# Which VectorE step each GpSimd step waits for, in a gated linear attention with a feed-forward block

## The chip, the cores and the metric

The kernel runs on one core of a Trainium2 chip. The metric is the device time of one execution in microseconds (us). A core has TensorE (PE in the profile, with its weight loads as PEld), VectorE (DVE), ScalarE (ACT), GpSimd (POOL) and SyncE (SP, which here only issues DMAs).

## The reference

Two parts follow each other. The first is a linear attention whose state is turned and damped by a complex gate at every time step, for 4 batches, 8 heads, 768 steps and a head dimension of 48. The second normalises the 384 channels of each step and applies a feed-forward block of 1536 hidden channels with a residual.

```python
# q, k, v, a_re, a_im: (4, 8, 768, 48)
mag = np.sqrt(a_re * a_re + a_im * a_im)
scale = np.minimum(mag, 0.999) / (mag + 1e-06)
a_re_n, a_im_n = (a_re * scale, a_im * scale)
for t in range(S):
    ar, ai = a_re_n[:, :, t, :, None], a_im_n[:, :, t, :, None]
    new_re = ar * S_re - ai * S_im
    new_im = ar * S_im + ai * S_re
    kv = np.einsum('bhd,bhe->bhde', k[:, :, t], v[:, :, t])
    S_re, S_im = (new_re + kv, new_im)
    y[:, :, t] = np.einsum('bhd,bhde->bhe', q[:, :, t], S_re)
x = y.transpose(0, 2, 1, 3).reshape(B, S, H * D)
xn = (x - mean(x)) / np.sqrt(var(x) + 1e-06) * g_ln      # over the 384 channels
out = x + np.maximum(xn @ w_ch1, 0.0) @ w_ch2
```

## The kernel before

**Tiling.** The 768 steps of a batch are cut into 6 chunks of 128, and two chunks make a pair: 4 batches times 3 pairs give 12 pairs P = 0 to 11 and 24 chunks n = 0 to 23. The gates' running products are turned into sums: logarithms of the magnitudes (`l`) and angles (`th`) are added up along time by matmuls with triangles of ones (`dec`, `ph`), then turned back by exponentials (`e`, `en`) and sines (`sin`, `cos`). q and k are multiplied with these (`qe`, `ke`, then `qs`, `ks`), and attention inside a chunk is a masked matmul, with a state `G` carried from chunk to chunk.

**Steps and names.** The function `pair_ops` adds every step of a pair by a name, with what it needs. The names that this text uses, with P the pair, n the chunk, and a last digit for a half:

- `ln`, `iv` (L459, L461, ScalarE), `r` (L463, a product of two SBUF tiles), `r2` (L472, its square), `u` (L473, ScalarE), `l` (L477), `lc` (L480, a clamp in place), `dec` (L488, TensorE), `th` (L496, ScalarE), `ph` (L503 and L507, TensorE), `sin` (L525, ScalarE), `qt` (L532, TensorE), `abs` (L544), `car` (L520).
- `ke`, `qe`, `ks`, `qs`: products of two SBUF tiles. All `tensor_tensor` calls run through one helper, so that `r`, `r2`, `ke`, `qe`, `ks`, `qs`, `atm`, `gs` and `G` all stand under L295.
- `kT`, `qT` (L613, transposes on TensorE), `ksT`, `qsT` (L292, their evacuation from PSUM), `am` (L636), `atm` (L652, evacuation of `am` with the mask), `gm` (L660), `G` and `gs` (the state), `y` (L697 and L700), `bn` (L707, L708, statistics), `x` (L714 or L717), `xr` (L724, between SBUF tiles), `xtr` and `xT` (L734, L292), `rstd` (L753 and L755 on GpSimd: an addition and a power).
- `mm1`, `relu`, `mm2` (L767, L779 or L781, L791: the feed-forward block), `oa` and `ot` (L796, L807 or L805: the output), `st` (L813, the store).
- `v` (L414, a cast), `wl.0` and `wl.1` (L369, L371: loads of the two weight matrices w1b and w2b, issued on GpSimd), `wc` (L385, scaling of w1b in SBUF), and `pad`, `car0`, `zrow`, `pick`, `mask`, `ident`: constants set by GpSimd at the start.

**Order.** A text, `PLAN`, lists all 1088 steps in one order, each with its engine: V is VectorE, G is GpSimd, A ScalarE, P TensorE, S SyncE, and a digit behind it is the PSUM bank. Each engine works through its own steps in that order. `tile_gateloop__then__metaformer_identity_kernel` hands it to `Graph.run`, which emits the steps. The waits that the data and the buffers ask for are added on their own. Beside these, a token may end in `@step`: then the first instruction of that step also waits for the last instruction of the named one, although it needs nothing of it.

```python
where, _, ops[name].behind = where.partition("@")
...
for op in steps:
    if op.behind:
        tc.add_manual_dep(made[op.name][0], made[op.behind][-1].name, info,
                          reason="turns at the shared port")
```

GpSimd has 103 steps, and 54 of them carry such a mark. Their targets are VectorE steps of every kind: 9 times `atm`, 6 times `ksT`, 5 times `bn`, 4 times `qsT`, and others. Many targets are the VectorE step just ahead of one that works between SBUF tiles. Since GpSimd works in order, a wait also holds everything behind it on GpSimd.

Of the kernel before, what the change touches and what calls it, by code (L numbers as in the profile page):

```python
# [53 lines left out]
warm.w17:P5 e.0.1:A1 k.1.1:S warm.w12:P3 lc.0.0:V iv.2.0:A lc.1.0:V dec.0.0:P7 qe.0.1.0:G@lc.0.0 car.0.0:V6 dec.1.0:P4
q.1.0:S car.0.1:V0 en.0.1:A1 r.2.0:V qrow:G warm.w16:P2 en.0.0:A7 ph.1.0:P2 e.1.0:A4 q.2.1:S ke.0.0.0:V e.0.0:A7
warm.28:P1 are.3.0:S r2.2.0:V en.1.0:A4 warm.19:P7 warm.w4:P1 uthc:V ke.0.1.0:V vf.1.0:S u.2.0:A warm.w0:P5 qe.0.0.0:V
warm.w40:P4 warm.w22:P7 car.1.0:V2 warm.w3:P7 k.1.0:S warm.5:P7 warm.w20:P5 l.2.0:V warm.w31:P7 warm.w23:P5 aim.3.0:S
warm.w21:P7 warm.w28:P1 qe.1.0.0:V tab.trig.3:A sin.0.1:A0 sin.0.0:A6 lc.2.0:V qt.0.1:P0 ks.0.1.1:V sin.1.0:A2 row.0:S
# [10 lines left out]
cos.3.0:A0 wc.0.0:V mm1.0.1.1:P2 vf.2.1:S wc.0.2:V x.2:A7 wc.2.2:V mm1.0.0.1:P0 wc.2.0:V relu.0.1:A2 wc.2.1:V bn.3:V5
mm1.0.0.0:P0 qe.2.0.0:G@wc.2.1 xtr.2:P3 aim.5.0:S x.3:V5 mm1.0.2.0:P6 ke.2.0.0:G@bn.3 xT.2:V3 xtr.3:P5 mm1.0.2.1:P6  # L70
xT.3:V5 tab.log.6:A u.3.0:A gs.3:V4 mm1.1.0.1:P2 qs.2.0.0:V relu.0.2:A6 mm1.1.1.0:P4 ks.2.0.0:V relu.0.0:A0
mm1.1.1.1:P4 ks.2.0.1:V mm1.1.0.0:P2 l.3.0:V ln.4.0:A mm1.1.2.1:P0 relu.1.1:A4 relu.1.0:V2 kT.5:P6 mm1.1.2.0:P0
iv.4.0:A ksT.5:V6 qT.5:P4 relu.1.2:A0 lc.3.0:V qT.4:P3 r.4.0:G@ksT.5 qsT.5:V4 kT.4:P5 qsT.4:A3 dec.3.0:P6 ksT.4:V5
# [5 lines left out]
mm2.1.2:P6 xr.1:G@qe.3.0.1 q.4.0:S xT.5:V5 ke.3.0.1:G ot.3:V7 mm1.2.0.0:P4 ot.1:V6 mm1.2.0.1:P4 aim.6.0:S rstd.2:G
qs.3.0.0:V k.4.0:S mm1.2.2.0:P2 tab.trig.7:A th.4.0:A ke.3.0.0:V mm1.2.2.1:P2 k.4.1:S relu.2.0:A4 ks.3.0.0:V ph.4.0:P6  # L80
st.1:S relu.2.2:A2 st.3:S l.5.0:V qT.6:P0 q.4.1:S abs.4.0:A6 dps.4:P1 kT.6:P5 v.3:G@ks.3.0.0 qsT.6:V0 mm1.2.1.0:P2
are.7.0:S th.5.0:A decc.4:V1 ksT.6:V5 kT.7:P0 sin.4.0:A6 vf.4.0:S dps.3:P4 mm1.2.1.1:P2 decc.3:V4 car.4.0:A6 ksT.7:V0
qT.7:P5 relu.2.1:A2 lc.5.0:V am.6:P6 r.6.0:G@ksT.7 qsT.7:V5 gm.6:P4 ph.5.0:P0 cos.4.0:A atm.6:V6 vf.4.1:S G.6:A4
am.7:P2 sin.5.0:A0 gm.7:P4 q.5.0:S ke.4.0.0:G@atm.6 atm.7:V2 y.6:P5 mm2.4.0:P7 abs.5.0:A0 ke.4.0.1:G mm2.5.0:P6
th.6.0:A G.7:V4 q.5.1:S y.7:P2 bn.6:V5 cos.5.0:A qe.4.0.0:G@G.7 mm2.5.1:P6 are.8.0:S bn.7:V2 x.6:A5 mm2.5.2:P6
aim.7.0:S x.7:V2 mm2.4.1:P7 ks.4.0.0:V k.5.1:S xtr.7:P2 xtr.6:P5 mm2.4.2:P7 tab.log.8:A ln.7.0:A xT.7:V2 ksT.8:S
dec.5.0:P0 xT.6:V5 r2.6.0:A qs.4.0.0:V kT.9:P4 e.5.0:A0 mm1.3.1.0:P2 v.4:G@xT.6 aim.8.0:S ksT.9:V4 en.5.0:A0 qT.8:P5
# [6 lines left out]
th.7.0:A q.6.1:S qT.10:P4 qsT.11:V5 vf.5.1:S xtr.8:P6 xr.7:G@l.7.0 cos.6.0:A ph.7.0:P0 xT.8:V6 ke.5.0.0:G@qsT.11
xT.9:V7 th.8.0:A qsT.10:V4 dps.6:P2 mm1.4.1.0:P6 sin.7.0:A0 ot.7:V3 mm1.4.0.1:P4 st.7:S rstd.4:G decc.6:A2 ks.5.0.0:V
r2.8.0:A mm1.4.0.0:P4 k.7.0:S vf.6.1:S lc.7.0:V mm1.4.1.1:P6 ke.6.0.0:G relu.4.0:A4 car.7.0:V0 aim.9.0:S kT.10:P3
kT.11:P2 abs.7.0:A0 ksT.10:V3 mm1.4.2.0:P4 relu.4.1:A6 ksT.11:V2 q.7.0:S am.10:P0 ks.6.0.1:V dec.7.0:P2
ks.6.0.0:G@ksT.11 atm.10:V0 q.7.1:S am.11:P6 mm1.4.2.1:P4 atm.11:V6 tab.log.10:A en.7.0:A2 mm2.9.0:P1 v.5:G@atm.10
e.7.0:A2 mm2.9.1:P1 relu.4.2:V4 qe.6.0.0:G@atm.11 ln.9.0:A y.10:P0 row.7:S gm.10:P2 vf.7.0:S ph.8.0:P6 u.8.0:A
bn.10:V0 aim.10.0:S G.10:V2 iv.9.0:A xr.8:G@bn.10 kT.13:P5 qs.6.0.0:V y.11:P4 vf.6.0:S x.10:A0 mm2.8.0:P2 abs.8.0:A6  # L100
xr.9:G bn.11:V4 mm2.9.2:P1 k.8.1:S r.9.0:G@qs.6.0.0 ksT.13:V5 xtr.10:P0 mm2.8.1:P2 x.11:V4 qsT.13:S mm2.8.2:P2
tab.trig.11:A sin.8.0:A6 xT.10:V0 ot.9:V1 qe.7.0.0:G xtr.11:P4 qT.12:P0 th.9.0:A xT.11:V4 st.9:S kT.12:P7 ot.8:V2
ke.7.0.1:G cos.8.0:A mm1.5.0.1:P4 qsT.12:V0 st.8:S are.10.0:S mm1.5.0.0:P4 cos.7.0:A l.8.0:V q.8.1:S ph.9.0:P0
# [759 lines left out]
```

## Time and profile before

| what | value |
|---|---|
| three runs | 185.98 us median (185.66 to 186.71) |
| span of the profiled execution, first to last instruction | 184.4 us |
| the profiled execution's own time | not given apart; the median stands 1.58 us above its span |
| PE busy | 175.1 us |
| DVE busy | 154.5 us, 273 instructions |
| ACT busy | 154.9 us |
| POOL busy | 111.2 us, 124 instructions |

The profile is of one execution. A line of the timeline gives the start in us from the span's beginning, the duration in us, the engine, the source line, the operation and its tiles as out<-in with shapes, how many instructions the line merges, and in brackets the idle time ahead of it and what ended it. The share of busy time of an engine that is not the bottleneck says little by itself: what counts is which wait ends last.

### The profile page before, as it was taken

The numbers are of one execution on the slowest core, as the hardware profiler recorded it, in microseconds if no ns is written. First come the engines' busy times: TensorE is split into PE (matmuls) and PEld (weight loads), VectorE is DVE, ScalarE is ACT, GpSimd is POOL, SyncE is SP. The second block draws the span as 40 slices with busy tenths as digits, with TensorE's granted clock in tenths as the row PEclk, the third lists the DMA queues.
The fourth block names the chain that finished last, engine by engine and source line by source line (L and its number), as shares of the span: only waits on it lengthen the run. The fifth ranks groups of instructions, "written<-read, shape, count | busy, mean of one in ns | idle before, by whom it ended". The sixth has DMA issues, their size and how long they took to land.

```text
span 184.4 us, 5011 instructions
## 1 busy us (share of the span) xinstructions
PE 175.1 (95%) x1971; PEld 138.2 (75%) x1971; DVE 154.5 (84%) x273; ACT 154.9 (84%) x217; POOL 111.2 (60%) x124
## 2 busy tenths in 40 slices
PE   5968989999999999999999999999999999999992
PEld 2545367789866886987887897887977979788871
DVE  2349999998888999999989989988988999977431
ACT  5899988989999999999999999999989973466320
POOL 7484068942586847799799966877959530280000
PEclk9999999999999999999999999999999999999999
DMA  5999999999986999989896999989699999992302
GB/s 142 305 201 230 231 187 187 231 252 203 231 176 138 252 256 217 197 222 198 183 242 126 229 221 191 214 187 215 148 233 165 207 135 201 242 199 90 108 0 85
DMA packets 128791, 35.39 MB, mean 192 GB/s; under 512 B 124800, under 2 KB 128000, under 8 KB 128768
## 3 DMA queue, kind: packets, MB, share of 16 engines
...
q8 instruction: 15, 0.25, 0.5%
...
## 4 chain that ended last, share of the span: by engine, by line
PE 74%; DVE 10%; SPq 7%; DMA 4%; issue 2%; POOL 1%; DVEq 0%
PE banks L767 24%; PE banks L791 23%; PE banks L613 6%; PE banks L636 5%; SPq L452 3%; SPq L404 3%; PE banks L507 3%; PE banks L488 3%; PE banks L697 2%; PE banks L660 2%; PE banks L700 2%; DMA k<-in_k_dram 2%; PE banks L734 2%; DMA q<-in_q_dram 2%; DVE qs L295 1%
## 5 line engine op out<-in xcount | busy, mean ns | idle before, releaser
L791 PE MATMUL banks<-w2b,h 128*128 128x384 bf16 (+2 forms) x300 | 53.0, 319 | 0.1
L767 PE MATMUL banks<-xT,w1b 128*128 128x256 bf16 x432 | 51.5, 273 | 0.0
L767 PEld LDWEIGHTS <-w1b 128*128 128x128 bf16 x432 | 46.1, 114 | 1.1 <-DVE stats L707 0.3
L779 ACT ACTIVATE h<-banks 128x1024 bf16<-128x1024 f32 x31 | 31.5, 1021 | 11.5 <-PE banks L767 11.3
L791 PEld LDWEIGHTS <-h 128*128 128x128 bf16 x300 | 26.9, 97 | 13.8 <-issue 0.2
L295 DVE TENSOR_TENSOR atm<-banks,mask 128x1024 bf16<-128x1024 f32 x24 | 28.9, 1219 | 3.6 <-PE banks L636 3.3
L295 POOL TENSOR_TENSOR r<-aim,are 128x768 f16<-128x768 f32 x9 | 16.5, 1832 | 8.6 <-DVE ksT L292 7.5
L831 ACT ACT_TABLE_LOAD x15 | 19.2, 1283 | 1.0 <-PEq L847 0.8
L295 POOL TENSOR_TENSOR qe<-q,e 128x384 bf16<-128x384 f32 (+1 forms) x14 | 16.2, 1157 | 4.7 <-ACT e L492 1.7
L826 PE MATMUL banks<-u_e 128*128 128x512 f16 x42 | 14.6, 436 | 2.4 <-POOL u_e L323 2.2
L724 POOL TENSOR_SCALAR xr<-x,mv 128x384 f32<-128x384 bf16 x13 | 8.5, 653 | 11.0 <-ACT x L714 4.7
L707 DVE BATCH_NORM_STATS2 stats<-banks 128x6 f32<-128x384 f32 x24 | 13.3, 556 | 1.2 <-PE banks L700 1.2
L636 PE MATMUL banks<-qsT,ksT 128*128 128x128 bf16 x192 | 14.3, 219 | 0.0
L477 DVE SCALAR_TENSOR_TENSOR l<-r,w 128x768 f16<-128x768 f16 (+1 forms) x13 | 11.7, 907 | 2.6 <-ACT r L473 2.6
L807 DVE SCALAR_TENSOR_TENSOR ot<-banks,rstd,xr 128x384 f32<-128x384 f32 (+2 forms) x18 | 10.4, 586 | 3.9 <-PE banks L791 3.3
L636 PEld LDWEIGHTS <-ksT 128*128 128x128 bf16 x192 | 12.2, 97 | 1.6 <-DVE ksT L292 0.2
L414 POOL TENSOR_SCALAR v<-vf 128x768 bf16<-128x768 f32 x9 | 9.5, 1058 | 5.6 <-DVE mv L708 2.7
L805 POOL TENSOR_TENSOR ot<-ot,x 128x384 f32<-128x384 f32 x7 | 7.0, 1006 | 9.1 <-DVE atm L295 7.9
L697 PE MATMUL banks<-v,atm 128*128 128x48 bf16 x192 | 12.0, 183 | 0.2 <-DVE atm L295 0.2
L459 ACT ACTIVATE w<-are 128x768 f32<-128x768 f32 (+1 forms) x13 | 10.2, 791 | 2.2 <-DMA are<-in_a_re_dram 2.2
L295 POOL TENSOR_TENSOR ke<-k,en 128x768 bf16<-128x768 f32 (+1 forms) x9 | 11.8, 1321 | 0.2
L697 PEld LDWEIGHTS <-atm 128*128 128x128 bf16 x192 | 10.8, 96 | 1.4 <-DVE atm L295 0.6
(100 smaller groups left out, 391.0 us busy)
## 6 DMA issues: line engine op xcount, KB each, us to landing
...
```

The source lines that it names most:

```text
L295: {"DVE": nc.vector, "POOL": nc.gpsimd}[eng(name)].tensor_tensor(**kw)
L477: nc.vector.scalar_tensor_tensor(out=S_("l"), in0=S_("r2"), scalar=0.5, in1=S_("w"), op0=ALU.mult, op1=ALU.add)
L613: nc.tensor.transpose(ps[:, h], T(nm, P)[:, c, h], ident)
L636: nc.tensor.matmul(ps[:, h], lhsT=T("ksT", n)[:, h], rhs=T("qsT", n)[:, h], start=True, stop=True)
L697: nc.tensor.matmul(ps[:, h], lhsT=T("atm", n)[:, h], rhs=T("v", P)[:, c, h], start=True, stop=nfirst)
L707: nc.vector.bn_stats(out=T("stats", n), in_=bank(f"y.{n}")[:, 0:DM])
L767: nc.tensor.matmul(ps[:, jj], lhsT=w1b[:, dc, ts(gi, JG * C)].rearrange("k (p j) -> k j p", j=JG)[:, jj], rhs=T("xT", P)[:, dc].rearrange( ...
L779: act(out=dst, in_=src, func=AF.Relu)
L791: nc.tensor.matmul(bank(f"o.{N}")[:, ws], lhsT=T("h", P)[:, j, ts(c, C)], rhs=w2b[:, j, ws], start=(j == 0), stop=(j == NJ - 1))
L807: nc.vector.scalar_tensor_tensor(out=o, in0=bank(f"o.{N}")[:, ws], scalar=T("rstd", P)[:, ds(c, 1)], in1=xs, op0=ALU.mult, op1=ALU.add)
L826: g.add(f"warm.w{i}", lambda i=i: nc.tensor.matmul(bank(f"warm.w{i}"), lhsT=u_e[:, 0, 0], rhs=u_e.rearrange("p c j t -> p (c j t)"), start ...
L831: g.add(f"tab.{nm}.{i}", lambda tab=tab: nc.scalar.preload_act_table_set(tab))
```

## The change

The order of the steps, their engines and their banks stay. Only the marks `@step` of GpSimd's steps change: each now names the last VectorE step ahead of it in the order that works between SBUF tiles without PSUM (`r`, `r2`, `l`, `lc`, `ke`, `qe`, `ks`, `qs`, `wc`, `xr`), and none where an earlier GpSimd step already waits for that one or a later one. VectorE steps that read PSUM (evacuations such as `ksT`, `qsT`, `atm`, `bn`, `G`) are no longer targets. 47 steps carry a mark instead of 54: 23 marks go, 16 are new, 26 name another step, and 5 stay. The first lines of the diff, and those around the four steps that the prediction costs:

```diff
-aim.1.0:S warm.w7:P0 tab.log.0:A ln.0.0:A pick:G@uth warm.w29:P5 are.2.0:S iv.0.0:A warm.w32:P0 car0.0:G warm.w10:P7
+aim.1.0:S warm.w7:P0 tab.log.0:A ln.0.0:A pick:G warm.w29:P5 are.2.0:S iv.0.0:A warm.w32:P0 car0.0:G warm.w10:P7
...
-qs.1.0.0:V qT.0:P6 warm.w34:P7 wl.0:G@qs.0.0.0 kT.1:P3 ksT.0:V4 qT.2:P2 k.2.0:S qsT.0:V6 qT.1:P5 ke.1.0.0:G q.2.0:S
+qT.0:P6 warm.w34:P7 wl.0:G@qs.1.0.0 kT.1:P3 ksT.0:V4 qT.2:P2 k.2.0:S qsT.0:V6 qT.1:P5 ke.1.0.0:G@qs.1.0.0 q.2.0:S
...
-rstd.1:G@atm.5 mm2.2.0:P1 ln.5.0:A row.3:S mm2.0.2:P4 l.4.0:V q.3.1:S v.2:A mm2.2.1:P1 G.3:G ot.0:V4 mm2.2.2:P1
+ln.5.0:A row.3:S mm2.0.2:P4 l.4.0:V q.3.1:S v.2:A mm2.2.1:P1 G.3:G@l.4.0 ot.0:V4 mm2.2.2:P1 iv.5.0:A lc.4.0:V k.3.1:S
...
-xr.5:V qe.5.0.0:G qT.9:P4 k.5.0:S qsT.8:V5 u.6.0:A mm1.3.1.1:P2 qsT.9:V4 rstd.3:G mm1.3.2.0:P0 relu.3.1:A2 l.6.0:V
-am.9:P4 k.7.1:S mm1.3.2.1:P0 qe.5.0.1:G iv.7.0:A atm.9:V4 mm1.3.0.1:P2 relu.3.2:A0 xr.4:G@qsT.9 mm1.3.0.0:P2 lc.6.0:V
+qs.4.0.0:V kT.9:P4 e.5.0:A0 mm1.3.1.0:P2 v.4:G@qs.4.0.0 aim.8.0:S ksT.9:V4 en.5.0:A0 qT.8:P5 xr.5:V qe.5.0.0:G@xr.5
+qT.9:P4 k.5.0:S qsT.8:V5 u.6.0:A mm1.3.1.1:P2 qsT.9:V4 rstd.3:G@xr.5 mm1.3.2.0:P0 relu.3.1:A2 l.6.0:V am.9:P4 k.7.1:S
+mm1.3.2.1:P0 qe.5.0.1:G@l.6.0 iv.7.0:A atm.9:V4 mm1.3.0.1:P2 relu.3.2:A0 xr.4:G@l.6.0 mm1.3.0.0:P2 lc.6.0:V
...
-k.6.1:S am.8:P2 vf.5.0:S mm2.6.0:P6 en.6.0:A4 r2.7.0:G@G.8 abs.6.0:V0 row.6:S mm2.6.1:P6 iv.8.0:A are.9.0:S car.6.0:V0
+e.6.0:A4 k.6.1:S am.8:P2 vf.5.0:S mm2.6.0:P6 en.6.0:A4 r2.7.0:G@qs.5.0.0 abs.6.0:V0 row.6:S mm2.6.1:P6 iv.8.0:A
```

Since the lines of the text break at other places, here are all 65 marks that differ, step by step in GpSimd's order, with the target before and after:

```
pick: uth > none, pad.ks.0: r2.0.0 > none, r2.1.0: none > r2.0.1, car0.1: uth > none, mask: r2.0.0 > none, zrow.0: uth > none,
pad.ks.1: r2.0.0 > none, qe.0.1.0: lc.0.0 > lc.1.0, wl.0: qs.0.0.0 > qs.1.0.0, ke.1.0.0: none > qs.1.0.0, qe.2.0.1: ksT.2 > none,
ngl: ksT.2 > none, r2.3.0: ksT.3 > none, wl.1: wc.1.1 > wc.1.2, ke.2.0.0: bn.3 > wc.2.1, r.4.0: ksT.5 > lc.3.0, rstd.1: atm.5 > none,
G.3: none > l.4.0, r.5.0: none > lc.4.0, xr.3: qe.3.0.0 > qe.3.0.1, v.3: ks.3.0.0 > l.5.0, r.6.0: ksT.7 > lc.5.0, ke.4.0.0: atm.6 > none,
qe.4.0.0: G.7 > none, v.4: xT.6 > qs.4.0.0, qe.5.0.0: none > xr.5, rstd.3: none > xr.5, qe.5.0.1: none > l.6.0, xr.4: qsT.9 > l.6.0,
r.7.0: none > lc.6.0, r2.7.0: G.8 > qs.5.0.0, r.8.0: abs.6.0 > none, G.9: gs.9 > none, ke.5.0.0: qsT.11 > l.7.0, ke.6.0.0: none > lc.7.0,
ks.6.0.0: ksT.11 > ks.6.0.1, v.5: atm.10 > none, qe.6.0.0: atm.11 > none, xr.8: bn.10 > none, xr.9: none > qs.6.0.0,
qe.7.0.1: qsT.12 > l.8.0, v.6: ke.7.0.0 > qs.7.0.0, rstd.5: none > qs.7.0.0, xr.11: bn.12 > lc.8.0, xr.10: qsT.14 > lc.8.0,
v.7: none > l.9.0, qe.8.0.0: lc.10.0 > lc.9.0, qe.9.0.1: none > ks.8.0.1, qs.8.0.1: none > ks.8.0.1, G.15: gs.15 > qs.8.0.0,
ot.12: none > qs.8.0.0, qe.9.0.0: xT.15 > none, rstd.7: atm.16 > qs.9.0.0, r2.11.0: G.16 > ks.9.0.0, qe.10.0.1: atm.17 > none,
rstd.8: bn.17 > none, ot.14: atm.18 > l.11.0, ot.15: none > qs.10.0.0, v.10: bn.19 > ks.10.0.0, ot.16: atm.21 > ks.11.0.0,
xr.19: gs.21 > ks.11.0.0, ot.17: atm.20 > none, G.21: x.20 > none, ot.18: xT.20 > none, xr.22: xr.21 > xr.20
```

More of the change, by code (lines that the diff above doesn't have):

```diff
@@ L54 @@
[L54 to L58, printed above, removed]
@@ L69 @@
[L69 to L73, printed above, removed]
@@ L79 @@
[L79 to L87, printed above, removed]
-xr.5:V qe.5.0.0:G qT.9:P4 k.5.0:S qsT.8:V5 u.6.0:A mm1.3.1.1:P2 qsT.9:V4 rstd.3:G mm1.3.2.0:P0 relu.3.1:A2 l.6.0:V
@@ L94 @@
[L94 to L103, printed above, removed]
@@ L104 @@
-qe.7.0.1:G@qsT.12 relu.5.0:A4 ksT.12:V7 mm1.5.1.1:P2 ke.7.0.0:V vf.7.1:S car.9.0:A0 mm1.5.1.0:P2 sin.9.0:A0 qs.7.0.0:V
-v.6:G@ke.7.0.0 mm1.5.2.1:P6 relu.5.1:A2 abs.9.0:V0 q.8.0:S rstd.5:G mm1.5.2.0:P6 ks.7.0.0:V are.11.0:S r2.9.0:A
-am.12:P2 am.13:P0 relu.5.2:A6 atm.12:V2 qs.7.0.1:G@ks.7.0.0 gm.12:P4 mm2.11.0:P5 G.12:A4 ksT.15:S mm2.11.1:P5
+xtr.0:P4 kT.3:P6 ksT.2:V7 ph.2.0:P2 G.1:V0 qe.2.0.1:G tab.trig.5:A th.3.0:A ksT.3:V6 am.2:P0 ngl:G sin.2.0:A2
+warm.w37:P7 v.1:G atm.2:V0 warm.13:P7 am.3:P6 xT.0:A4 qt.2.0:P2 r2.3.0:G x.1:A5 gm.2:P4 atm.3:V6 ph.3.0:P0 cos.2.0:A2
@@ new lines @@
+ot.2:G bn.5:V0 mm2.1.0:P6 en.4.0:A2 x.4:V4 mm2.3.1:P7 e.4.0:A2 st.2:S r2.5.0:V vf.3.1:S mm2.1.1:P6 qe.3.0.0:V x.5:A0
+row.4:S xtr.4:P2 qe.3.0.1:V iv.6.0:A mm2.3.2:P7 vf.3.0:S xr.3:G@qe.3.0.1 xT.4:V2 xtr.5:P5 u.5.0:A mm2.1.2:P6
+xr.1:G@qe.3.0.1 q.4.0:S xT.5:V5 ke.3.0.1:G ot.3:V7 mm1.2.0.0:P4 ot.1:V6 mm1.2.0.1:P4 aim.6.0:S rstd.2:G qs.3.0.0:V
+k.4.0:S mm1.2.2.0:P2 tab.trig.7:A th.4.0:A ke.3.0.0:V mm1.2.2.1:P2 k.4.1:S relu.2.0:A4 ks.3.0.0:V ph.4.0:P6 st.1:S
+relu.2.2:A2 st.3:S l.5.0:V qT.6:P0 q.4.1:S abs.4.0:A6 dps.4:P1 kT.6:P5 v.3:G@l.5.0 qsT.6:V0 mm1.2.1.0:P2 are.7.0:S
```

120 lines of the change are left out of this document (72 added, 48 removed).

## The prediction, made before the changed kernel had run

> **What bounds the kernel now.** I read the page's shares first, then its 40 slices, and last the timeline around every GpSimd step whose wait changes.
>
> ```profile
> span 184.4 us, 5011 instructions
> ...
> PE 175.1 (95%) x1971; PEld 138.2 (75%) x1971; DVE 154.5 (84%) x273; ACT 154.9 (84%) x217; POOL 111.2 (60%) x124
> ```
>
> ```profile
> PE   5968989999999999999999999999999999999992
> ...
> PEclk9999999999999999999999999999999999999999
> ```
>
> TensorE is the bound: 95% of the span, and in the 40 slices (4.61 us each) it reads 9, that is 90% or more, from the eighth to the last but one, at the full granted clock. GpSimd is 60% busy. So a GpSimd step that comes earlier wins next to nothing after about 35 us. One that comes later costs as soon as it has used up the slack towards the TensorE step that needs it, and TensorE then has little idle time in which to win that back: delays add up.
>
> **How the two engines meet.** Before the parts can be priced, this trace has to say what a GpSimd step costs when it meets a VectorE step between two SBUF operands.
>
> ```profile
> 63.13 0.95 DVE L477 SCALAR_TENSOR_TENSOR l<-r,w 128x768 f16<-128x768 f16 x1
> ...
> 63.31 1.47 POOL L414 TENSOR_SCALAR v<-vf 128x768 bf16<-128x768 f32 x1 [0.59 <-DVE ks L295]
> ...
> 97.00 0.83 POOL L414 TENSOR_SCALAR v<-vf 128x768 bf16<-128x768 f32 x1
> ...
> 134.75 0.95 DVE L295 TENSOR_TENSOR ke<-k,en 128x768 bf16<-128x768 f32 x1
> ...
> 150.24 1.38 POOL L414 TENSOR_SCALAR v<-vf 128x768 bf16<-128x768 f32 x1 [2.71 <-DVE mv L708]
> ...
> 150.85 1.58 DVE L295 TENSOR_TENSOR qe<-q,e 128x768 bf16<-128x768 f32 x1
> ```
>
> `v` takes 0.83 us undisturbed. Started 0.18 us into `l`, it took 1.47 and ended 0.70 after `l` (64.78 against 64.08): it stood still until `l` was over, less about 0.13 that it did anyway. So GpSimd's time is its own plus what is left of the VectorE step, less 0.13. The other way round, `qe` came while `v` had the lead and took 1.58 where the same shape takes 0.95 (`ke`): 0.63 longer, which is the rest of `v` (151.62 - 150.85) less 0.14. Hence the first effect of the change: a GpSimd step that used to start beside the VectorE step and stand still now waits for its end. It starts some 0.9 later, is 0.64 shorter, and ends about 0.25 later (0.1 for the wait, 0.13 for the head start lost). VectorE's step, which was ahead, wins nothing. That is small, but it can happen at up to 42 steps: 26 whose target moves and 16 that had no wait and get one.
>
> The waits that vanish (23) I cost at zero: memsets at the start and steps that stood directly behind other GpSimd work. Everything queued behind a waiting GpSimd step moves with it, the two weight loads among it.
>
> **Four places where the later end reaches TensorE.** I take 0.1 us from a VectorE step's end to the GpSimd start that waits for it.
>
> First, `wl.0` (the load of w1b) waits for `qs.1.0.0`.
>
> ```profile
> 24.30 0.95 DVE L295 TENSOR_TENSOR qs<-qe,trig 128x1536 bf16<-128x1536 bf16 x1
> 24.69 1.00 POOL L369 DMA_DIRECT2D w1b<-in_moe_w_ch_dram  x1 [8.24 <-DVE qs L295]
> ...
> 27.47 3.10 POOL L295 TENSOR_TENSOR ks<-ke,trig 128x1536 bf16<-128x1536 bf16 x1
> ...
> 31.21 1.81 POOL L295 TENSOR_TENSOR r<-aim,are 128x768 f16<-128x768 f32 x1 [0.63 <-ACT are L461]
> ...
> 33.88 0.79 ACT L525 ACTIVATE trig<-banks 128x768 bf16<-128x768 int16 x1
> ...
> 34.77 0.49 PE L532 MATMUL banks<-qrow,pick 1*128 1x384 f16 x2
> ```
>
> The old target `qs.0.0.0` ended at about 24.38 and the issue followed 0.31 later; the new one ends at 25.25, so `wl.0`, `ke.1.0.0` and `ks.1.0.0` behind it come 0.87 later. `ks.1.0.0` ends at 31.44, past 31.21, where `r.3.0` started on ScalarE's word: 0.64 of the 0.87 is slack and `r.3.0` comes 0.2 late. It feeds `th.3.0` on ScalarE, behind which stands `sin.2.0` (33.88), which ends 0.10 before TensorE's `qt.2.0`. **+0.15.**
>
> Both weight loads are issued on GpSimd; `wl.1` (w2b) waits for `wc.1.2` instead of `wc.1.1`.
>
> ```profile
> 36.84 1.13 DVE L385 TENSOR_SCALAR w1b<-w1b,ngl 128x512 bf16<-128x512 bf16 x4
> ...
> 38.02 0.84 POOL L371 DMA_DIRECT2D w2b<-in_moe_w_ch_dram  x1 [1.09 <-DVE w1b L385]
> ...
> 50.07 1.14 PE L791 MATMUL banks<-w2b,h 128*128 128x384 bf16 x6
> ```
>
> ```profile
> w1b<-in_moe_w_ch_dram POOLq DMA_DIRECT2D x1, 1152.0 KB, 10.1
> w2b<-in_moe_w_ch_dram POOLq DMA_DIRECT2D x1, 1152.0 KB, 11.3
> ```
>
> w1b landed at 24.69 + 10.1 = 34.8 and is first touched at 36.84: its 0.87 is covered. w2b landed at 49.3, and `mm2.0.0` uses it from 50.07; one `wc` step (1.13 / 4 = 0.28) and the 0.15 of above later it lands near 49.7. Zero, covered by 0.75 us of slack; if its landing slipped by more, the rest would show on TensorE.
>
> Second, `G.3` waits for `l.4.0`.
>
> ```profile
> 52.17 0.95 DVE L477 SCALAR_TENSOR_TENSOR l<-r,w 128x768 f16<-128x768 f16 x1
> 52.19 1.62 POOL L295 TENSOR_TENSOR G<-gt,dec 128x384 bf16<-128x384 f32 x1
> ...
> 53.56 0.46 DVE L480 TENSOR_SCALAR l<-l 128x768 f16<-128x768 f16 x1
> ...
> 54.07 1.82 POOL L295 TENSOR_TENSOR r<-aim,are 128x768 f16<-128x768 f32 x1 [0.26 <-ACT are L461]
> ...
> 54.17 0.81 PE L488 MATMUL banks<-l,u_e 128*128 128x384 f16 x4
> ...
> 86.90 0.83 POOL L295 TENSOR_TENSOR G<-gt,dec 128x384 bf16<-128x384 f32 x1 [0.24 <-DVE gt L295]
> ```
>
> With the 0.15 from before, `l.4.0` ends at 53.27, `G.3` runs from 53.37 to 54.20 (0.83, as at 86.90), and `lc.4.0`, due at 53.71, now is the one that meets it: held 54.20 - 53.71 - 0.13 = 0.36, it ends at 54.42. TensorE's `dec.4.0` started 0.15 behind it and starts at 54.47 at the earliest: 0.30 late, **+0.15** more.
>
> Third, `qe.5.0.0` and, in effect, all behind it wait for `xr.5`, and `qe.5.0.1` for `l.6.0`.
>
> ```profile
> 76.03 0.41 DVE L724 TENSOR_SCALAR xr<-x,mv 128x384 f32<-128x384 bf16 x1
> ...
> 76.08 1.14 POOL L295 TENSOR_TENSOR qe<-q,e 128x384 bf16<-128x384 f32 x1
> ...
> 77.59 0.70 POOL L755 TENSOR_TENSOR rstd<-rstd,half_n 128x2 f32<-128x2 f32 x1
> ...
> 77.73 0.95 DVE L477 SCALAR_TENSOR_TENSOR l<-r,w 128x768 f16<-128x768 f16 x1
> ...
> 79.46 0.57 POOL L724 TENSOR_SCALAR xr<-x,mv 128x384 f32<-128x384 bf16 x1
> ...
> 80.18 1.12 DVE L807 SCALAR_TENSOR_TENSOR ot<-banks,rstd,xr 128x384 f32<-128x384 f32 x2
> ...
> 81.15 0.34 PE L660 MATMUL banks<-v,ks 128*128 128x48 bf16 x7
> ```
>
> `qe.5.0.0` would start at 76.44 + 0.30 + 0.1 = 76.84 and take 0.91 (1.14 less the 0.23 that it stood). Then the power of `rstd.3`, which started 0.14 ahead of `l.6.0` in this trace, starts 0.1 behind it and stands for most of it: about 0.7 more. So `qe.5.0.1` ends near 80.4 and `xr.4` near 81.0 where it ended at 80.03. `ot.4`, the first of the two at 80.18, needs `xr.4`; it ends about 81.75 and holds bank 7, which TensorE's `gm.8` needs at 81.45 (81.15 + 0.30). **+0.4**; it is nothing if the power still starts first.
>
> Fourth, `r2.7.0` waits for `qs.5.0.0` instead of `G.8`.
>
> ```profile
> 82.02 0.95 DVE L295 TENSOR_TENSOR qs<-qe,trig 128x1536 bf16<-128x1536 bf16 x1
> ...
> 82.25 2.05 POOL L295 TENSOR_TENSOR r<-r 128x768 f16<-128x768 f16 x1 [0.31 <-DVE G L295]
> ...
> 84.33 0.84 ACT L473 ACTIVATE r<-r 128x768 f16<-128x768 f16 x1
> ...
> 88.11 0.85 ACT L496 ACTIVATE th<-r 128x768 f16<-128x768 f16 x1
> ...
> 89.07 0.49 PE L507 MATMUL banks<-th,u_th 128*128 128x384 f16 x2
> ...
> 137.82 1.47 POOL L295 TENSOR_TENSOR r<-r 128x768 f16<-128x768 f16 x1 [1.57 <-DVE G L295]
> ```
>
> `qs.5.0.0` ends at 82.97 + 0.70; `r2.7.0` (1.47 alone) runs from 83.8 to 85.3, 1.0 later than the 84.30 of before. `u.7.0` on ScalarE took it up 0.03 after its end, and ScalarE works without a break up to `th.7.0` (ends 88.96), 0.11 ahead of `ph.7.0`. So `ph.7.0` is 1.0 to 1.05 late where TensorE was already 0.7: **+0.35**.
>
> Behind 90 us the delays on GpSimd reach 1.3 to 1.9, but TensorE is 1.05 late itself, and what is left (0.3 to 0.9) lies within the slack of each consumer that I followed. `ot.16`, `xr.19` and `ot.17`, whose targets were evacuations near the end, come 2 to 4 us earlier (from the same working) and win nothing, since the end is set by TensorE.
>
> Sum: 0.15 + 0.15 + 0.4 + 0.35 = 1.05 us on the span of 184.4, so 185.45. The 185.98 median of the three runs (185.66 to 186.71) stands 1.58 above that span; I take this as what lies around the span and the profiled execution as typical: 185.98 + 1.05 = **187.0**. With the third term at nothing the fourth is 0.3 and the sum 0.6; with one more hold like `qe`'s (0.63) on the path it is 1.7: its own range is 186.6 to 187.7. About 0.5% (0.93 us) is what a measurement of this kernel can tell from no change.
>
> **The rivals.** *Absorbed.* Terms three and four need a chain of four GpSimd steps to be late in a row. If they vanish, 0.3 is left: 186.3. For it: GpSimd idles for 40% of the span. Against: TensorE has nothing idle there.
>
> *More holds.* A late GpSimd step is still running when VectorE's next step between SBUF operands is due, as `v.10` did to `qe.11.0.0`. The new order invites it wherever two such VectorE steps stand close: `qe.7.0.1` sits between `l.8.0` and `ke.7.0.0`, `v.7` between `l.9.0` and `l.10.0`, `v.10` between `ks.10.0.0` and `qe.11.0.0`. With two of the three on the path at 0.63 each: 1.05 + 1.26 = 2.3, so 188.3. Against: after 90 us VectorE has some slack. The Trainium skill, SBUF — State Buffer, section Who interferes with whom, says that the order of issue decides, and that the later of the two stands for the whole instruction. By that rule, moving GpSimd behind one VectorE step just hands the block to the next, and the trace agrees in that one hold of 0.63.
>
> *The race goes (the other side).* `l.4.0` started 0.02 us ahead of `G.3`. In an execution where `G.3` is first, `l.4.0` is held 0.68, `lc.4.0` comes at 54.24 behind `r.5.0` (54.07, 1.82 long) and is held to 55.9: it ends 2.1 later and `dec.4.0` starts 2.0 later. The change makes `G.3` wait, so this can't occur. If more than half of the timed runs of before lose that race and the profiled one won it, the result is 185.98 - 2.0 + 1.05 = 185.0, faster. Against: three times within 1.05 us show no gap of 2.
>
> **How the numbers follow.** Forecast 0.45, of which 0.09 lies within 0.5%; absorbed 0.21; more holds 0.18; the race 0.16. Slower by over 0.5%: 0.36 + 0.18 = 0.54. Within: 0.09 + 0.21 = 0.30. Faster: 0.16. The likeliest gives 187.0. The range runs from just under the race's 185.0 to just over the holds' 188.3: 184.9 to 188.5.
>
> **What would show it.** Right: `v` behind `l` takes 0.83 instead of 1.47 and ends some 0.25 later; `lc.4.0` grows from 0.46 to about 0.7; the power of `rstd.3` grows from 0.70 to about 1.4; `r2.7.0` takes 1.47, `ot.4` and `gm.8` come later by more than what TensorE brought along. TensorE's busy time stays and the span grows. Wrong: those steps shorten and TensorE's steps at 54, 81 and 89 us come no later, or a new wait of TensorE on VectorE or ScalarE stands at a place not named here.

## The result and the profile after

| | before | after |
|---|---|---|
| median of 22 runs each | 186.18 us (185.66 to 187.62) | 187.07 us (186.53 to 188.51) |
| ratio | | 1.0047 (95% interval 1.003 to 1.0064) |
| span of the profiled execution | 184.4 us | 184.8 us, its time 186.86 us |

The change costs 0.87 us (the interval of the ratio makes it 0.56 to 1.19). The limit named in the prediction, 0.5% or 0.93 us, lies inside that interval: the runs say that the kernel became slower, and cannot say whether by more or less than that limit. The ratios in this text leave out executions in a second, slower state (one of `before_again`, one of `no_marks`); the medians still hold them.

The page of the changed kernel, its shares and slices:

```profile
span 184.8 us, 5008 instructions
...
PE 174.8 (95%) x1971; PEld 137.8 (75%) x1971; DVE 155.9 (84%) x273; ACT 155.1 (84%) x217; POOL 105.0 (57%) x124
...
PE   5959879999999999999999999999999999999993
...
PEclk9999999999999999999999999999999999999999
```

TensorE is the bound as before, at the same clock. GpSimd is busy 6.2 us less (111.2 to 105.0) and VectorE 1.4 us more (154.5 to 155.9): GpSimd stands less inside its instructions, and nobody is served by that. The span hides part of the loss. The last output step on VectorE ends at 182.09 us instead of 181.34, 0.75 later; the span grew by 0.4 only, because the last store took less time in this execution.

The timeline of the changed kernel, at the places that the prediction named (start, duration, engine, line, operation, tiles; in brackets the idle time ahead and what ended it):

```profile
25.54 1.00 POOL L369 DMA_DIRECT2D w1b<-in_moe_w_ch_dram  x1 [9.15 <-DMA row<-e]
...
31.38 1.82 POOL L295 TENSOR_TENSOR r<-aim,are 128x768 f16<-128x768 f32 x1
...
34.83 0.49 PE L532 MATMUL banks<-qrow,pick 1*128 1x384 f16 x2
...
52.23 0.95 DVE L477 SCALAR_TENSOR_TENSOR l<-r,w 128x768 f16<-128x768 f16 x1
53.26 0.83 POOL L295 TENSOR_TENSOR G<-gt,dec 128x384 bf16<-128x384 f32 x1 [1.18 <-DVE l L477]
53.62 0.68 DVE L480 TENSOR_SCALAR l<-l 128x768 f16<-128x768 f16 x1
54.35 0.49 PE L488 MATMUL banks<-l,u_e 128*128 128x384 f16 x2
...
64.42 0.83 POOL L414 TENSOR_SCALAR v<-vf 128x768 bf16<-128x768 f32 x1 [1.46 <-DVE l L477]
...
77.92 0.95 DVE L477 SCALAR_TENSOR_TENSOR l<-r,w 128x768 f16<-128x768 f16 x1
78.12 1.31 POOL L755 TENSOR_TENSOR rstd<-rstd,half_n 128x2 f32<-128x2 f32 x1
80.31 0.68 POOL L724 TENSOR_SCALAR xr<-x,mv 128x384 f32<-128x384 bf16 x1
81.02 1.14 DVE L807 SCALAR_TENSOR_TENSOR ot<-banks,rstd,xr 128x384 f32<-128x384 f32 x2 [0.48 <-POOL xr L724]
81.69 0.36 PE L660 MATMUL banks<-v,ks 128*128 128x48 bf16 x8 [0.20 <-DVE ot L807]
...
82.56 1.02 DVE L295 TENSOR_TENSOR qs<-qe,trig 128x1536 bf16<-128x1536 bf16 x1
83.72 1.47 POOL L295 TENSOR_TENSOR r<-r 128x768 f16<-128x768 f16 x1 [0.96 <-DVE qs L295]
85.22 0.84 ACT L473 ACTIVATE r<-r 128x768 f16<-128x768 f16 x1 [0.86 <-POOL r L295]
...
89.01 0.85 ACT L496 ACTIVATE th<-r 128x768 f16<-128x768 f16 x1
89.91 0.48 PE L507 MATMUL banks<-th,u_th 128*128 128x384 f16 x2
```

Read it place by place. `wl.0` is issued 0.85 later than before, and `qt.2.0` starts at 34.83 instead of 34.77. `G.3` takes 0.83 instead of 1.62, but now `lc.4.0` meets it and takes 0.68 instead of 0.46, and `dec.4.0` stands behind that. The power of `rstd.3` starts 0.20 into `l.6.0` and takes 1.31 instead of 0.70; `xr.4` ends at 80.99, `ot.4` has waited 0.48 for it, and TensorE waits 0.20 for `ot.4`. `r2.7.0` takes 1.47 instead of 2.05, but starts 1.47 later than before (83.72 against 82.25), and ScalarE's `u.7.0` waits 0.86 for it. `v.3` is the small case: 0.83 instead of 1.47, ended at 65.25 instead of 64.78. Of these 0.47 us, 0.24 are `l.5.0` itself, which starts at 63.37 instead of 63.13; 0.23 are the price of the wait.

One measure compares kernels in this whole text: how much later a TensorE step starts than in the profiled execution of before, less the delay of `kT.1`, the transposes of `ks` near 25 us. Ahead of it the kernels of the table differ in few marks or none, and executions of one kernel differ there by up to 0.89 (the rows of before and of v3_late, each run twice). The kernel with no marks and the one with 93 are not in the table. `dps.6` is the TensorE step right behind `ph.7.0` (L597). Times in us, from the traces:

| kernel | `kT.1` | `qt.2.0` | `dec.4.0` | `gm.8` | `dps.6` | `mm2.9.0` | `mm2.8.0` | `mm1.11.0.0` |
|---|---|---|---|---|---|---|---|---|
| before, a second time | -0.21 | 0 | 0 | 0 | 0 | -0.21 | -0.09 | +0.19 |
| after | -0.02 | +0.08 | +0.21 | +0.57 | +0.86 | +0.65 | +0.77 | +0.77 |
| four_only | -0.14 | +0.09 | +0.21 | +0.58 | +0.87 | +0.66 | +0.78 | +1.01 |
| four_undone | +0.36 | 0 | +0.01 | +0.01 | +0.01 | -0.01 | +0.10 | +0.10 |
| qe5_only | +0.21 | 0 | 0 | +0.36 | +0.41 | +0.20 | +0.32 | +0.44 |
| r27_only | -0.18 | 0 | 0 | 0 | +0.23 | +0.02 | +0.14 | +0.14 |
| r27_abs | -0.20 | +0.01 | +0.01 | +0.01 | +1.11 | +0.89 | +1.01 | +1.02 |
| gone_only | -0.43 | 0 | +0.54 | +0.54 | +0.53 | +0.32 | +0.46 | +0.79 |
| wl1_free | -0.16 | 0 | +0.01 | +0.01 | +0.01 | +0.02 | +0.02 | +0.10 |
| v3_late | +0.62 | 0 | +0.01 | +0.01 | +0.01 | +0.02 | +0.01 | +0.29 |
| v3_late, a second time | -0.27 | 0 | 0 | 0 | 0 | +0.01 | 0 | +0.11 |

### The profile page after: what moved, and what is told of

Its sections match the earlier page's. It is cut to its first block, busy times and chain, and to the rows that moved or that the text cites. A ratio compares the mean times of both kernels' runs of the same rounds, so it can differ in the third digit from the quotient of the medians.

```text
span 184.8 us, 5008 instructions
## 1 busy us (share of the span) xinstructions
PE 174.8 (95%) x1971; PEld 137.8 (75%) x1971; DVE 155.9 (84%) x273; ACT 155.1 (84%) x217; POOL 105.0 (57%) x124
## 4 chain that ended last, share of the span: by engine, by line
PE 77%; DVE 8%; SPq 6%; issue 2%; DMA 2%; ACT 2%; POOL 1%; DVEq 0%; POOLq 0%
PE banks L767 25%; PE banks L791 23%; PE banks L613 6%; PE banks L636 5%; PE banks L507 3%; SPq L452 3%; SPq L404 3%; PE banks L488 3%; PE banks L697 2%; DMA k<-in_k_dram 2%; PE banks L660 2%; PE banks L700 2%; PE banks L734 2%; DVE qs L295 2%; PE banks L503 2%
## 5 line engine op out<-in xcount | busy, mean ns | idle before, releaser
L295 DVE TENSOR_TENSOR atm<-banks,mask 128x1024 bf16<-128x1024 f32 x24 | 28.9, 1219 | 3.7 <-PE banks L636 3.3
L295 POOL TENSOR_TENSOR r<-aim,are 128x768 f16<-128x768 f32 x9 | 16.4, 1819 | 9.0 <-ACT are L461 6.2
L295 POOL TENSOR_TENSOR qe<-q,e 128x384 bf16<-128x384 f32 (+1 forms) x14 | 15.1, 1075 | 5.9 <-ACT h L779 1.6
L826 PE MATMUL banks<-u_e 128*128 128x512 f16 x42 | 13.9, 419 | 2.4 <-POOL u_e L323 2.2
L807 DVE SCALAR_TENSOR_TENSOR ot<-banks,rstd,xr 128x384 f32<-128x384 f32 (+2 forms) x18 | 10.4, 588 | 4.4 <-PE banks L791 3.3
L724 POOL TENSOR_SCALAR xr<-x,mv 128x384 f32<-128x384 bf16 x13 | 7.7, 593 | 10.0 <-DVE stats L707 5.3
L414 POOL TENSOR_SCALAR v<-vf 128x768 bf16<-128x768 f32 x9 | 8.0, 893 | 8.6 <-DVE ks L295 3.3
L295 POOL TENSOR_TENSOR ke<-k,en 128x768 bf16<-128x768 f32 (+1 forms) x9 | 11.9, 1323 | 0.1
L697 PEld LDWEIGHTS <-atm 128*128 128x128 bf16 x192 | 10.7, 96 | 1.5 <-DVE atm L295 0.6
L292 DVE COPY ksT<-banks 128x1024 bf16<-128x1024 bf16 x16 | 10.9, 685 | 1.1 <-PE banks L613 0.8
```

The source lines that it names most:

```text
L292: nc.vector.tensor_copy(out=dst, in_=src)
L295: {"DVE": nc.vector, "POOL": nc.gpsimd}[eng(name)].tensor_tensor(**kw)
L697: nc.tensor.matmul(ps[:, h], lhsT=T("atm", n)[:, h], rhs=T("v", P)[:, c, h], start=True, stop=nfirst)
L826: g.add(f"warm.w{i}", lambda i=i: nc.tensor.matmul(bank(f"warm.w{i}"), lhsT=u_e[:, 0, 0], rhs=u_e.rearrange("p c j t -> p (c j t)"), start ...
```

## The experiments

The theory: the loss arises at the four places of the prediction, and the other marks that differ do nothing. The main rivals: the loss is spread over all 42 GpSimd steps with a new or moved mark (more holds), or the vanished marks carry it. Ten of these 42 marks (`ke.1.0.0`, `ke.2.0.0`, `rstd.3`, `xr.4`, `ke.5.0.0`, `rstd.5`, `xr.10`, `qs.8.0.1`, `ot.12`, `xr.19`) name a step for which an earlier GpSimd step waits already: they add no wait, though the rule as it is told above would give them none.

Each ratio is taken against runs of the kernel before that were made beside the run (their medians are 185.99 to 186.09 us), so it can differ a little from a quotient with 186.18.

**four_undone and four_only.** Twelve marks make up the four places, those behind each place that belong to it among them. `four_undone` is the changed kernel with these twelve as before, `four_only` is the kernel before with these twelve changed. Here and below a diff shows only the tokens that differ, put side by side; the first is that of `four_only`:

```diff
-wl.0:G@qs.0.0.0  ke.1.0.0:G
+wl.0:G@qs.1.0.0  ke.1.0.0:G@qs.1.0.0
-rstd.1:G@atm.5  G.3:G  r.5.0:G
+rstd.1:G  G.3:G@l.4.0  r.5.0:G@lc.4.0
-qe.5.0.0:G  rstd.3:G  qe.5.0.1:G  xr.4:G@qsT.9  r.7.0:G
+qe.5.0.0:G@xr.5  rstd.3:G@xr.5  qe.5.0.1:G@l.6.0  xr.4:G@l.6.0  r.7.0:G@lc.6.0
-r2.7.0:G@G.8  r.8.0:G@abs.6.0
+r2.7.0:G@qs.5.0.0  r.8.0:G
```

> The changed kernel, with the marks of before put back at the four places that the prediction priced (wl.0 and ke.1.0.0; G.3, r.5.0 and rstd.1; qe.5.0.0, rstd.3, qe.5.0.1, xr.4 and r.7.0; r2.7.0 and r.8.0: 12 of the 65 marks; the other 53 stay as changed). Theory A, the loss sits at these four places because only there a later GpSimd step reaches TensorE: the time goes back to that of before, ratio 1.000 (0.998 to 1.002). Theory B, the loss is spread over all GpSimd steps that end about 0.25 us later: some 53/65 of 0.87 us stays, ratio 1.004. Theory C, the loss comes from marks that are gone: ratio 1.004 to 1.005.

> The kernel of before, with the new marks at the four places alone (12 marks). Theory A: all of the loss is there, 0.75 to 1.05 us, ratio 1.004 to 1.006. Theory B: 12/65 of it, ratio 1.001. Theory C: none, ratio 1.000.

`four_undone`: 186.45 us, ratio 1.0013 (0.9997 to 1.003). `four_only`: 186.99 us, ratio 1.0042 (1.0023 to 1.0062). The same rows of the two timelines, `kT.1` and `gm.8`, first four_undone, then four_only:

```profile
25.47 0.61 PE L613 MATMUL banks<-ident,ks 128*128 128x128 bf16 x8
...
81.51 0.36 PE L660 MATMUL banks<-v,ks 128*128 128x48 bf16 x8
```

```profile
24.96 0.61 PE L613 MATMUL banks<-ident,ks 128*128 128x128 bf16 x8
...
81.58 0.36 PE L660 MATMUL banks<-v,ks 128*128 128x48 bf16 x8 [0.20 <-DVE ot L807]
```

From `kT.1` to `gm.8` it is 56.04 us in the one and 56.62 in the other (before: 81.15 - 25.11 = 56.04), and only the second waits 0.20 for `ot.4`. The row of `four_only` in the table is that of the changed kernel to 0.01 us up to `mm2.8.0`. So twelve marks carry the delay. With the 53 others alone TensorE is not late up to 96 us and 0.10 late after it, which is less than the 0.19 by which the kernel before differs from itself at `mm1.11.0.0`; the timed runs of `four_undone` can't tell that from nothing. The split of the first 0.21 between places one and two is read from the traces of the changed kernel and of four_only; neither place has a run of its own.

**qe5_only, r27_only and r27_abs.** Place three and place four one at a time, in the kernel before; the third moves `r2.7.0` further, behind the next evacuation:

```diff
-qe.5.0.0:G
+qe.5.0.0:G@xr.5
```

> The kernel of before with one mark of the third place: qe.5.0.0 waits for xr.5. In the profile, TensorE's gm.8 (81.15 us in before) is to be compared with the steps ahead of it, so that a shift of the start does not count. Theory A (the power of rstd.3 falls behind l.6.0, is held for some 0.7 us and makes xr.4, ot.4 and gm.8 late): gm.8 0.35 to 0.45 later than its neighbours. Rival: the mark of qe.5.0.1 on l.6.0 is what costs; then at most 0.1 here.

```diff
-r2.7.0:G@G.8
+r2.7.0:G@qs.5.0.0
```

> The kernel of before with the one mark of the fourth place, r2.7.0 on qs.5.0.0. Against the steps ahead of them, so that a shift of the start does not count: theory A 0.25 to 0.35 us later at ph.7.0 or at dps.6 behind it, nothing at gm.8. Rival (the fourth place costs only on top of the third): 0.

```diff
-r2.7.0:G@G.8  r.8.0:G@abs.6.0
+r2.7.0:G@abs.6.0  r.8.0:G
```

> The kernel of before with one step made to wait longer: r2.7.0 waits for abs.6.0 instead of G.8 (and the mark of r.8.0 on abs.6.0, now without use, is gone); in before, abs.6.0 ends 1.74 us after G.8, and r2.7.0 is then no longer stretched, so it ends about 1.15 us later. Theory A (r2.7.0 has no slack: u.7.0, ScalarE without a break, th.7.0, ph.7.0): 1.1 us at ph.7.0 and dps.6, and 0.9 to 1.15 us in the time, ratio 1.005 to 1.006. Rival (the delay is taken up before TensorE or won back behind 96 us, where TensorE stood 0.2 us): ratio 1.000 to 1.003.

`qe5_only`, one execution: `gm.8` is 0.36 late, as large as the step from `dec.4.0` to `gm.8` in the changed kernel (0.57 - 0.21). One mark of five makes the whole of place three. Its timeline:

```profile
76.79 0.92 POOL L295 TENSOR_TENSOR qe<-q,e 128x384 bf16<-128x384 f32 x1 [0.57 <-ACT e L492]
...
78.08 1.37 POOL L755 TENSOR_TENSOR rstd<-rstd,half_n 128x2 f32<-128x2 f32 x1
...
81.71 0.36 PE L660 MATMUL banks<-v,ks 128*128 128x48 bf16 x8 [0.19 <-DVE ot L807]
```

`r27_only`, one execution: 0.23 at `dps.6` and nothing before it. That is a little under what was expected. In the changed kernel place four added 0.29 on top of a TensorE that was already late. `r27_abs`: 186.93 us, ratio 1.0048 (1.0029 to 1.0066), 1.11 us at `dps.6`. One step of GpSimd with a worse target costs as much as the whole change, since `u.7.0` and `th.7.0` on ScalarE and `ph.7.0` on TensorE follow it with no more than the 0.11 of slack that the prediction read.

**Where 0.21 comes back.** In all six rows of the table that come late to `dps.6`, the delay falls by 0.21 or 0.22 at `mm2.9.0` (0.12 to 0.14 of it is lost again by `mm2.8.0`). The same fall and return stand in the row of the kernel before, run a second time, which was late nowhere. This is `mm2.9.0` and the matmuls ahead of it (`mm1`), in the first trace of before and in that of r27_only:

```profile
95.84 0.82 PE L767 MATMUL banks<-xT,w1b 128*128 128x256 bf16 x6
96.71 1.46 PE L791 MATMUL banks<-w2b,h 128*128 128x384 bf16 x8
```

```profile
95.90 0.82 PE L767 MATMUL banks<-xT,w1b 128*128 128x256 bf16 x6
96.55 1.46 PE L791 MATMUL banks<-w2b,h 128*128 128x384 bf16 x8
```

From the one to the other 0.87 pass in before, 0.65 in r27_only (and 0.66 in the changed kernel): by these starts TensorE stood 0.22 in the profiled execution of before, and whoever comes later uses it up. `mm2.9.0` writes a bank that `atm.10` reads first, and `atm.10` ends 0.05 before it starts. What makes `atm.10` late is a chain on GpSimd. The timelines of before and of before_again (the kernel before, unchanged):

```profile
91.31 1.21 POOL L753 TENSOR_SCALAR rstd<-mv 128x2 f32<-128x2 f32 x1
...
94.96 0.56 DVE L295 TENSOR_TENSOR ks<-ke,trig 128x768 bf16<-128x768 bf16 x1 [0.28 <-POOL ke L295]
```

```profile
91.09 0.98 POOL L753 TENSOR_SCALAR rstd<-mv 128x2 f32<-128x2 f32 x1
...
94.52 0.56 DVE L295 TENSOR_TENSOR ks<-ke,trig 128x768 bf16<-128x768 bf16 x1
```

Both start at the same moment after `kT.1`; the first op of `rstd.4` stands behind VectorE's `ks.5.0.0` in both, but once it takes 1.21 and once 0.98. Then `ke.6.0.0` on GpSimd and `ks.6.0.1` on VectorE come 0.22 later, and `atm.10` with them. Among the twelve profiled executions of kernels with this stretch in order (those of the table and before), eight took 1.21 and four 0.98, before the one and before_again the other. So the fall depends on which execution of before the others are compared with; it is no gain of the change. But of the six profiled executions that are not late there, five took 1.21: if the timed runs of before are like these, most of them have this stall too, and part of what the four places cost comes back in the time as well. The interval of the timed runs (0.56 to 1.19) is too wide to tell.

> The kernel of before itself, under a label of its own, as a measure of what an unchanged kernel gets: 1.000, and within 0.998 to 1.002 if the spread of the start is all that moves these ratios.

`before_again`: 186.19 us, ratio 1.0005 (0.9986 to 1.0024): what these runs say of a kernel against itself.

**gone_only and wl1_free.** The first takes away the 23 marks that vanish and leaves the rest as before. The second frees the load `wl.1`:

```diff
-pick:G@uth  pad.ks.0:G@r2.0.0  car0.1:G@uth
+pick:G  pad.ks.0:G  car0.1:G
...
-rstd.1:G@atm.5  ke.4.0.0:G@atm.6  qe.4.0.0:G@G.7
+rstd.1:G  ke.4.0.0:G  qe.4.0.0:G
...
```

> The kernel of before, with only the 23 marks taken away that the change takes away; no mark is new or moved. Theory A: the steps behind them are held by their data, their engine's order or TensorE's end, so nothing changes, ratio 1.000 (0.998 to 1.002). Theory C: the whole loss, ratio 1.004 to 1.005. A hidden gain of the removal, which the four places would then outweigh: ratio under 0.998.

```diff
-wl.1:G@wc.1.1
+wl.1:G
```

> The kernel of before without the mark of wl.1 on wc.1.1: the load of w2b is issued right behind xr.0, at about 37 us instead of 38.0. In the runs so far w2b landed 10.4 to 12.6 us after its issue, between 48.8 and 50.1 us, and mm2.0.0 uses it from 50.1: its slack is 0 to 1.3 us. If the landing bounds some executions, the median falls a little: ratio 0.998 to 0.9995, and this would be a version under both. If it bounds none: 1.000. If the issue meets VectorE's wc steps and is held: 1.000 to 1.002, with the landing where it was.

`gone_only`: 186.06 us, ratio 1.001 (0.9991 to 1.003). The timed runs show no cost, but its profiled execution came 0.54 late at `dec.4.0`, from a place that is none of the four. The timeline and the view of the DMAs:

```profile
50.18 1.62 PE L791 MATMUL banks<-w2b,h 128*128 128x384 bf16 x9 [0.37 <-DMA w2b<-in_moe_w_ch_dram]
```

```profile
w2b<-in_moe_w_ch_dram POOLq DMA_DIRECT2D x1, 1152.0 KB, 12.5
```

w2b was issued at 37.60, earlier than the 38.02 of before, and landed at 50.1 instead of 49.3. In the changed kernel it was issued at 38.35, later, and landed at 48.8, earlier (10.4 us). The landing does not follow the issue in step. `wl1_free`, with its issue at 36.74 and its landing at 48.1, is at 186.09, ratio 1.0009 (0.9992 to 1.0026): no gain shows there.

**no_marks and every_ahead.** What is the mark worth at all? `no_marks` is the kernel before without any of its 54 marks; in `every_ahead` every GpSimd step but the first ten waits for the VectorE step directly ahead of it in the order, of whatever kind (93 marks):

```diff
-pad.ks.0:G@r2.0.0  wl.0:G@qs.0.0.0  r.6.0:G@ksT.7
+pad.ks.0:G         wl.0:G           r.6.0:G
...
```

> The kernel of before without any of GpSimd's 54 marks. Theory A with the hold working both ways: GpSimd runs ahead, its steps are still running when VectorE's next step between SBUF operands is due, and VectorE is held for the rest of each; the trace of before worked forward by that rule has 22 VectorE steps held for over 0.3 us, 22 us in all, of which 14.5 us reach TensorE: about 200.7 us, ratio 1.06 to 1.09. Rival, only GpSimd pays when the two meet and VectorE does not: 0.99 to 1.003. Rival, VectorE is held but has the slack for most of it: 1.01 to 1.03.

```diff
-pad.ks.0:G@r2.0.0  r2.1.0:G         v.0:G
+pad.ks.0:G@r2.0.1  r2.1.0:G@r2.0.1  v.0:G@r2.0.1
...
```

> The kernel of before with every GpSimd step behind 9 us waiting for the VectorE step directly ahead of it in the order, of whatever kind, evacuations too. Theory A (a late GpSimd step costs once its slack is used up, and waiting for evacuations, which do not hold GpSimd, buys nothing): the trace of before worked forward gives 7.7 us more, about 193.8 us, ratio 1.035 to 1.045. Rival (GpSimd stands idle for 40% of the time and takes up such waits): 1.000 to 1.01.

`no_marks`: 203.54 us, ratio 1.093 (1.0898 to 1.0962). That is just above the 1.06 to 1.09 that were expected, and the composition is another one. Its page and its groups by line and form:

```profile
PEclk9999995799999999999999999999999999999999
...
L292 DVE COPY ksT<-banks 128x1024 bf16<-128x1024 bf16 x16 | 10.9, 684 | 0.9 <-PE banks L613 0.7
...
L480 DVE TENSOR_SCALAR l<-l 128x768 f16<-128x768 f16 x11 | 11.3, 1036 | 0.0
```

The same two groups in the kernel before:

```profile
L292 DVE COPY ksT<-banks 128x1024 bf16<-128x1024 bf16 x16 | 10.9, 684 | 0.9 <-PE banks L613 0.5
...
L480 DVE TENSOR_SCALAR l<-l 128x768 f16<-128x768 f16 x11 | 4.0, 367 | 0.0
```

The timeline of no_marks:

```profile
16.34 1.00 POOL L369 DMA_DIRECT2D w1b<-in_moe_w_ch_dram  x1
30.47 1.62 POOL L295 TENSOR_TENSOR ke<-k,en 128x768 bf16<-128x768 f32 x1 [13.14 <-DMA k<-in_k_dram]
...
31.88 0.81 ACT L492 ACTIVATE e<-banks 128x768 bf16<-128x768 f32 x1 [4.38 <-DMA row<-e]
...
32.74 0.48 PE L660 MATMUL banks<-v,ks 128*128 128x48 bf16 x8 [3.58 <-ACT e L492]
...
103.93 2.05 POOL L295 TENSOR_TENSOR ke<-k,en 128x768 bf16<-128x768 f32 x1
104.40 1.80 DVE L480 TENSOR_SCALAR l<-l 128x768 f16<-128x768 f16 x1
```

Two things are lost. The load `wl.0`, which waited for `qs.0.0.0` until 24.69, goes out at 16.34, together with the small early loads; GpSimd then waits 13.14 us for `k`. ScalarE waits 4.38 for the small transfer `row`, which SyncE issues at 28.77 instead of 22.31, and TensorE waits 3.58 for ScalarE: `gm.0` starts 3.6 late (32.74 against 29.16), and by `qt.2.0` it is 5.7 (40.48 against 34.77). This collision is read from one profile; no run of its own parts it from the rest. The other 11 to 12 us come later, and here GpSimd goes first: `lc` has one SBUF operand only, and its mean rises from 367 ns in before to 1036 ns. At 104.40 it meets `ke`, which ends at 105.98, and it ends at 106.20. In all, 24 VectorE steps are held by over 0.1 us, 19.6 us together. `ksT`, which reads PSUM, has 684 ns with and without marks.

`every_ahead`: 192.43 us, ratio 1.0341 (1.0312 to 1.0371), 6.4 us, just below the 1.035 to 1.045 that were expected. Here waits cost, and 15 VectorE steps are held all the same, for 5.8 us: a late GpSimd step can meet the next VectorE step.

**v3_late, twice.** One late step where the prediction saw slack: `v.3` waits for the evacuation behind `l.5.0`.

```diff
-v.3:G@ks.3.0.0
+v.3:G@ksT.6
```

> The kernel of before with one step made late by more than any of the change: v.3 waits for ksT.6 (ends at 65.75 us) instead of ks.3.0.0 (63.22): it starts 2.5 us later and, undisturbed, ends 1.9 us later; GpSimd then stands idle until r.6.0 in before anyway. Theory A (a GpSimd step costs only once its slack towards TensorE is used up, and v.3's is not): ratio 1.000 (0.998 to 1.002). Theory B (every later GpSimd step costs): 1.004 or more.

> The same kernel as v3_late, which gave a ratio of 1.0023 (1.0007 to 1.004) although no step of its profile between 25 and 172 us had moved against its neighbours. If that excess is the spread of the start (the loads of the first 15 us land 0.6 us earlier or later from one execution to the next): 0.999 to 1.002 now. If v.3 itself costs: 1.002 to 1.003 again.

The first time 186.45 us, ratio 1.0023 (1.0007 to 1.004), outside of what was expected; yet its row of the table shows nothing from `kT.1` to `mm2.8.0`, and its `kT.1` is 0.62 late. The second time 185.93, ratio 0.9995 (0.9977 to 1.0014), with `kT.1` 0.27 early. In the profiled execution the excess stood there before the edited step, and the same kernel did not have it again. So twelve runs with an interval of 0.3% can miss by about as much, which is why the table counts from `kT.1`.

No kernel here beat the one before.

## Why the prediction came out, step by step

**The size.** 187.0 forecast, 187.07 measured. The increment was put at 1.05 and is 0.87 (0.56 to 1.19), and the kernel before was put at 185.98, the median of three runs, where 22 give 186.18. The one is 0.18 too high and the other 0.20 too low: that the sum fits to 0.07 is luck. The call is less good than the number: 0.54 was given to slower by over 0.5%, and the middle of the measurement, 0.47%, lies just inside that limit.

**The four terms.** As forecast and as the trace has them: `qt.2.0` 0.15 and 0.08; `dec.4.0` 0.15 and 0.13; `gm.8` 0.4 and 0.36; `ph.7.0` with `dps.6` 0.35 and 0.29. Sum 1.05 and 0.86. Every term has the right place, cause and sign, and each was a little too large. That 0.86 meets the 0.87 of the timed runs proves little: the trace is 0.65 late at `mm2.9.0` and 0.77 at `mm1.11.0.0`. The first was mis-sized by its own rows: `r.3.0` 0.2 late, less the 0.10 by which `sin.2.0` was ahead, is 0.1, and it came to 0.08. In the second, `lc.4.0` was held as said (0.68, forecast about 0.7), but started 0.09 before the 53.71 that I gave it. In the third, the power took 1.31 where 1.4 was said. In the fourth, `th.7.0` came 0.90 later (89.01 against 88.11) where 1.0 to 1.05 was said.

**The law of the two engines** held. The power of `rstd.3`: 0.70 alone, plus what was left of `l.6.0` (78.87 - 78.12 = 0.75), less 0.13, is 1.32; measured 1.31.

**The costs at zero** held, one of them by luck as much as by cover. The vanished marks cost nothing that the timed runs show (ratio 1.001, at most 1.003). The 0.75 us of slack of w2b held in the changed kernel, but among the kernels of the table the landing lies anywhere from 47.9 to 50.1, by more than that slack, so it was never a safe cover. The cover of w1b shrank too: in the changed kernel it landed at 36.3 (10.7 us after its issue) and is touched at 36.90, 0.6 later, where the prediction read 2.0.

**Absorbed** is refuted: place three alone makes 0.36, and 0.77 of the delay stays in TensorE to the end, as was argued from its lack of idle time. What came back, 0.21, was a stall in the profiled execution of before that I had not seen.

**More holds** happened, and apart from that of `lc.4.0`, which is place two, they cost nothing that shows. VectorE was held in five steps by over 0.1 us before, 1.3 us in all, and in eight after, 2.3 us in all. The hold of 0.63 did not go away, it moved to the next step. Before, `qe.11.0.0` had it; after, `ke.11.0.1` (L295, 1.18 instead of 0.55):

```profile
151.60 0.95 DVE L295 TENSOR_TENSOR qe<-q,e 128x768 bf16<-128x768 f32 x1
151.83 1.41 POOL L414 TENSOR_SCALAR v<-vf 128x768 bf16<-128x768 f32 x1 [3.33 <-DVE ks L295]
152.47 1.18 DVE L295 TENSOR_TENSOR ke<-k,en 128x384 bf16<-128x384 f32 x1
```

`v.10` waits for `ks.10.0.0` as its mark says, then stands behind `qe.11.0.0`, and `ke.11.0.1` stands behind it. That is what the Trainium skill, SBUF — State Buffer, section Who interferes with whom, says of the order of issue, and the trace agrees. Of the other two spots that the prediction named, `ke.7.0.0` is held 0.34 instead of 0.12, and `l.10.0` 0.25 as before. But in this trace the holds after 90 us did not reach TensorE: TensorE's delay does not grow between `dps.6` and `mm1.11.0.0`, but for the 0.12 that every row with the fall at `mm2.9.0` has.

**The race** is not in the data. In all nine profiled executions in which `G.3` and `rstd.1` have the marks of before, `l.4.0` is 0.02 ahead. One of them, before_again's, took 186.12 us, near the median of 186.18 of the 22 runs: no 2 us are hidden there. In gone_only `G.3` did start first, by 0.45, and `lc.4.0` then came 0.05 ahead of `r.5.0` and ran its 0.35: the price of 2 us that I gave this rival does not even follow whenever `G.3` is first. Its timeline:

```profile
51.30 0.83 POOL L295 TENSOR_TENSOR G<-gt,dec 128x384 bf16<-128x384 f32 x1
51.74 1.19 DVE L477 SCALAR_TENSOR_TENSOR l<-r,w 128x768 f16<-128x768 f16 x1
53.60 0.35 DVE L480 TENSOR_SCALAR l<-l 128x768 f16<-128x768 f16 x1
53.65 1.99 POOL L295 TENSOR_TENSOR r<-aim,are 128x768 f16<-128x768 f32 x1 [1.53 <-ACT are L461]
```
